# Routing search: counts by seventeen 32-column matmuls, one expansion from PSUM, the remaining capacity added by a matmul

## The chip, the cores and the metric

The kernel runs on one core of one Trainium2 chip. The metric is the device time of one execution in microseconds (us). Three runs of the kernel before took 782.95, 785.60 and 788.19 us, median 785.6 us. PE is TensorE (PEld its weight loads), DVE is VectorE, ACT is ScalarE, POOL is GpSimd, SP the engine that issues the plain loads.

## What is computed

Local and global attention over 8 batches gives 4608 tokens of 512 numbers. A gate gives each token 8 logits. A greedy routing by falling logit then gives each token one of 8 experts, each with room for 576 tokens, and each expert runs a two-layer net over its tokens.

```python
cap = N // E                                  # 4608 // 8 = 576
logits = x @ w_gate
order = np.argsort(-logits.flatten())
for idx in order:
    tok, e = (int(idx) // E, int(idx) % E)
    if assigned[tok] >= 0 or counts[e] >= cap:
        continue
    assigned[tok] = e
    counts[e] += 1
for e in range(E):
    mask = assigned == e
    h = np.maximum(x[mask] @ w1[e], 0.0)
    out[mask] = h @ w2[e]
```

## The kernel before, in words

Attention runs first. Then `experts` runs eight passes, one for each expert in the order in which the experts fill up. A pass is `ffn(ph)`: 16 groups of 12 matmuls (L853, moving 272 columns) into PSUM tile `H`, each evacuated by ACT (`hh`) and by DVE (`hl`), then 4 groups of 24 matmuls (L881, moving 512 columns) into `Y`.

Which expert fills next, and with which tokens, is found by `Routing.phase`. For seven of the eight phases it calls `search`, eight rounds of a 16-ary search for the logit at which some expert is full. A round is a chain between PE and DVE:

- A 0/1 table `G` (128 partitions x 34 token groups x 16 thresholds) is multiplied with the one-hot table `oh` (34 x 8 experts): five matmuls into PSUM tile `R` (variable `A`), four of them eight token groups wide (128 columns of `G`, 64 of `oh`) and the second one two groups wide (32 columns, 16). Only the diagonal blocks of the result are wanted.
- DVE masks out the diagonal blocks (`am`, from PSUM and the constant `dj`), reduces `am` to `C` (a ninth slice of `am` holds the remaining capacity of each expert), and spreads `C` over the 16 thresholds (`ce`, from `C` and `dk`).
- One matmul with the constant `big` sums `ce` over the partitions into PSUM tile `R2` (here called the sum matmul), DVE scans that for the threshold (`pm`), and `cand` builds the next `G`. A small `x` (the keys less the threshold found) is also made on DVE, ahead of `am` in its queue.

Phase 0 runs by itself after attention, since no expert can start without it. The routing of phase n+1 is woven into pass n. Every routing instruction on DVE goes through the helper `issue` (L405) and every routing matmul through `mm` (L468), so these two lines carry all of them in the profile; the tiles tell them apart.

The order is written out in advance: Tile follows the program order, and a small planner sets that order. `V.now` is its estimate of PE's time: each FFN matmul adds 117 ns (L853) or 216 ns (L881), each routing matmul 30 ns. `V.busy` is its estimate of when DVE is free: an instruction of n elements takes 130 ns plus 0.55 or 1.05 ns an element. `search` yields `ready()` = `V.busy` + 400 ns before its matmuls, so `step` places FFN matmuls on PE until the estimate has passed, and only then the routing matmul. What stands between a routing matmul and the next is so a fixed number of FFN matmuls, which cover the DVE chain as long as it is fast enough; PE takes its queue in order, so if DVE is late, PE stands still. The splits of the weights (`w1l`, `w2l`, L704) run on POOL all through the passes.

Of the kernel before, what the change touches and what calls it, by code (L numbers as in the profile page):

```python
# [21 lines left out]
E = 8  # L22
# [353 lines left out]
CU = 64  # L376
# [6 lines left out]
class Queue:  # L383
    """VectorE as the program order sees it: each instruction moves on an estimate of when the engine is free."""
# [24 lines left out]
class Routing:  # L409
# [10 lines left out]
    def prepare(s):  # L420
# [25 lines left out]
        s.dj = cf[:, CMISC:CMISC + 8]  # L446
        nc.vector.memset(s.am[:, 8], 0.0)
        nc.vector.memset(s.am[:16, 8], CU * (0.5 - CAP))
        nc.vector.memset(s.asgv, 0.0)
        nc.vector.tensor_copy(s.act, s.wt)  # L450
        s.dk = consts.tile([128, 16], F16, name="dk")
        nc.vector.tensor_copy(s.dk, cf[:, CMISC + 8:CMISC + 24])

    def begin(s, ctx):
# [4 lines left out]
        for n, w, dt in (("m", [34], F32), ("f", [34], I32), ("u", [34], I32), ("hi", [34], I32), ("mv", [34], F32),  # L459
                         ("v", [34, E], BF16), ("mo", [34], BF16), ("oh", [34, E], BF16), ("G", [34, 16], BF16),  # L460
                         ("asgv", [34], F32), ("act", [E], F32), ("am", [9, E], F16)):
# [5 lines left out]
    def mm(s, out, *args, **kw):  # L467
        s.nc.tensor.matmul(out, *args, **kw)  # L468
        s.V.now += 30
        s.V.busy = max(s.V.busy, s.V.now + 200)  # L470
# [36 lines left out]
    def search(s):  # L507
        nc = s.nc
        for it in range(NIT):
            yield -1  # L510
            yield s.V.ready()
            A = s.ps.tile([128, 8, E], F32, name="R")
            for i, j in enumerate((0, 4, 1, 2, 3)):
                n = 8 if j < 4 else 2
                s.mm(A[:16 * n, :n], s.G[:, 8 * j:8 * j + n].rearrange("p a b -> p (a b)"),
                                 s.oh[:, 8 * j:8 * j + n], start=(i == 0), stop=(i == 4))
# [6 lines left out]
            else:  # L523
# [15 lines left out]
            s.mm(p, s.big, ce, start=True, stop=True)  # L539
# [8 lines left out]
    def phase(s, ph):  # L548
# [40 lines left out]
        if more:  # L589
# [3 lines left out]
            s.V.tensor_tensor(ohg, s.oh, g[:, :, None].to_broadcast([128, 34, E]), op=ALU.mult)  # L593
        if not last:
# [63 lines left out]
        if more:  # L658
            s.V.tensor_tensor(rem, rem, cl[:16], op=ALU.min)
# [338 lines left out]
```

## Time and profile before

| what | us |
|---|---|
| median of three runs | 785.6 |
| lowest and highest | 782.95, 788.19 |
| span of the profiled execution | 797.1 |
| attention, up to the last gate reduction | 237.9 |
| first routing, up to the first FFN matmul | 282.8 |
| first L871 matmul of pass 0 and of pass 5 | 315.1, 658.0 |
| first L871 matmul of passes 6 and 7 | 709.1, 760.4 |

The profile gives the profiled execution's span and no other time of it; the span is 11.5 us above the median of the runs. A pass without routing takes 51.3 us (658.0 to 709.1 and 709.1 to 760.4). From pass 0 to pass 5 it is 68.6 us a pass (342.9 us for five), since routing stands in the same PE queue. In a timeline row stand start, duration, engine, line, operation, tiles, shape, count, and in brackets the engine's idle time before it with what ended it.

### The profile page before, as it was taken

What the parts mean: (1) busy time and instruction counts of PE and PEld (TensorE: products, weight loads), DVE (VectorE), ACT (ScalarE), POOL (GpSimd) and SP (SyncE); (2) the same over time, 40 slices, a digit from 0 to 9 for tenths busy, and PEclk for the clock granted to TensorE, in tenths of its full rate; (3) what the DMA queues carried; (4) which work ended last, traced back from release to release, by engine and by line L of the source; (5) the groups of instructions that cost most, each with busy time, mean ns of one, the idle gap of its engine ahead of it and who ended that gap; (6) DMA issues with size and microseconds to landing.
All of it is one profiled execution on the core that took longest, in us unless ns stands there. A gap on an engine that the chain in (4) does not pass through costs nothing.

```text
span 797.1 us, 19772 instructions
## 1 busy us (share of the span) xinstructions
PE 717.4 (90%) x7876; PEld 578.2 (73%) x7876; DVE 504.9 (63%) x1817; ACT 312.6 (39%) x849; POOL 319.3 (40%) x314
## 2 busy tenths in 40 slices
PE   7899999999982599989988988989899789999994
PEld 6677777777751488779668867858877787987973
DVE  6787887778776888579668667876875752121210
ACT  4656675756640143144223333332331323433410
POOL 5221111111000362566546655563653654574610
PEclk9999999999995579999999999999999999999998
DMA  9998889878310430601430440350341323332000
GB/s 354 406 342 295 327 296 318 314 261 313 142 69 1 145 123 1 264 35 34 143 135 28 150 157 18 120 178 28 120 162 44 119 57 123 132 119 87 28 20 36
DMA packets 32412, 120.42 MB, mean 151 GB/s; under 512 B 6720, under 2 KB 6976, under 8 KB 24128
## 3 DMA queue, kind: packets, MB, share of 16 engines
q1 hardware_dynamic: 22080, 67.78, 23.2%
q0 software_dynamic: 10240, 51.39, 18.6%
q8 instruction: 62, 1.02, 0.5%
q14 instruction: 30, 0.25, 0.1%
HBM read 101.32 MB, written 17.83 MB: 149 GB/s over the span
## 4 chain that ended last, share of the span: by engine, by line
PE 76%; DVE 14%; issue 3%; DMA 3%; POOL 1%; ACT 1%; another core or an unknown queue 0%; POOLq 0%; SPq 0%; ACTq 0%; DVEq 0%
PE Y L881 20%; PE H L853 19%; PE S L134 8%; PE R L468 6%; PE O L162 5%; PE T L150 4%; DVE r_G L405 3%; PE H L726 3%; PE S L195 2%; PE T L259 2%; DVE r_ce L405 2%; PE O L234 2%; PE T L224 2%; PE Y L871 2%; DMA w1r<-in_w_dram,widx 1%
## 5 line engine op out<-in xcount | busy, mean ns | idle before, releaser
L853 PE MATMUL H<-xh,w1h 128*128 128x272 f32 x512 | 153.4, 300 | 9.3 <-DVE hl L405 9.3
L853 PE MATMUL H<-xl,w1h 128*128 128x272 f32 x512 | 152.9, 299 | 0.0
L853 PE MATMUL H<-xh,w1l 128*128 128x272 f32 x512 | 152.5, 298 | 0.0
L405 DVE SCALAR_TENSOR_TENSOR hl<-H,hh 128x272 fp32r<-128x272 f32 x128 | 55.2, 435 | 90.4 <-ACT hh L855 59.7
L145 ACT ACTIVATE p<-p,nm 128x128 f32<-128x128 f32 x256 | 82.0, 394 | 67.5 <-DVE ls L165 34.7
L855 ACT ACTIVATE hh<-H 128x272 fp32r<-128x272 f32 x128 | 51.0, 398 | 145.7 <-PE H L853 138.8
L853 PEld LDWEIGHTS H<-xh,w1h 128*128 128x128 f32 x512 | 100.0, 195 | 10.6 <-DVE hl L405 10.2
L881 PE MATMUL Y<-w2h,hh 128*128 128x512 f32 x256 | 105.6, 412 | 0.0
L704 POOL TENSOR_TENSOR w2l<-w2r,w2h 128x512 fp32r<-128x512 f32 x64 | 82.0, 1304 | 58.8 <-ACT w2h L703 55.8
L704 POOL TENSOR_TENSOR w1l<-w1r,w1h 128x512 fp32r<-128x512 f32 x60 | 78.3, 1321 | 66.3 <-ACT w1h L703 66.1
L881 PE MATMUL Y<-w2h,hl 128*128 128x512 f32 x256 | 104.5, 408 | 0.0
L881 PE MATMUL Y<-w2l,hh 128*128 128x512 f32 x256 | 104.3, 407 | 0.0
L853 PEld LDWEIGHTS H<-xl,w1h 128*128 128x128 f32 x512 | 100.0, 195 | 0.3
L853 PEld LDWEIGHTS H<-xh,w1l 128*128 128x128 f32 x512 | 100.1, 195 | 0.0
L86 POOL COPY qz<-q 64x544 f32<-64x544 f32 x60 | 38.4, 639 | 151.6 <-DMA q<-in_qk_dram 118.5
L826 ACT ACTIVATE y<-Y 128x512 f32<-128x512 f32 (+1 forms) x40 | 23.1, 594 | 134.7 <-PE Y L881 83.1
L134 PE MATMUL S<-qk,qz 128*64 128x128 f32 x1024 | 70.5, 279 | 4.9 <-DVE qz L86 2.8
L134 PEld LDWEIGHTS S<-qk,qz 128*64 128x64 f32 x1024 | 54.9, 136 | 17.4 <-issue 11.3
L733 POOL DMA_INDIRECT out_dram<-y,idx x40 | 41.5, 1036 | 61.6 <-ACT y L826 29.7
L141 DVE CUSTOM_DVE_ANT_0 p<-S,mask 128x128 f32<-128x128 f32 x256 | 58.8, 286 | 6.4 <-PE S L134 4.5
L881 PEld LDWEIGHTS Y<-w2h,hh 128*128 128x128 f32 x256 | 49.2, 192 | 13.9 <-issue 4.2
L703 ACT ACTIVATE w1h<-w1r 128x512 fp32r<-128x512 f32 x64 | 38.3, 627 | 47.1 <-DMA w1r<-in_w_dram,widx 47.1
(165 smaller groups left out, 1273.1 us busy)
## 6 DMA issues: line engine op xcount, KB each, us to landing
vw<-in_vw_dram SPq DMA_DIRECT2D x32, 1040.0 KB, 8.3
qk<-in_qk_dram SPq DMA_DIRECT2D x32, 432.0 KB, 5.8
q<-in_qk_dram SPq DMA_DIRECT2D x32, 272.0 KB, 5.6
xd<-xs SPq DMA_DIRECT2D x8, 1024.0 KB, 7.1
xd<-xg SPq DMA_DIRECT2D x64, 8.0 KB, 5.9
xg<-xd,idx POOLq DMA_INDIRECT x40
out_dram<-y,idx POOLq DMA_INDIRECT x40
mask<-in_mask_dram SPq DMA_DIRECT2D x1, 512.0 KB, 5.7
```

Source lines behind the costliest of these rows:

```text
L86: eng.tensor_copy(z[r, :, h, :], q[r].rearrange("p (j i) -> p j i", i=32))
L134: nc.tensor.matmul(st[64 * r:64 * r + 64, c, :], z[:, j].rearrange("p h i -> p (h i)"), kw[:, k0:k0 + 128], start=True, stop=True)
L141: nc.vector.tensor_tensor_reduce(s.p[:, c, :], st[:, c, :], mask[:, 4 * s.u + c, :], 1.0, -BIG, ALU.add, ALU.max, nm[:, c:c + 1])
L145: nc.scalar.activation(s.p[:, c, :], s.p[:, c, :], AF.Exp, bias=nm[:, c:c + 1], scale=SCALE)
L162: nc.tensor.matmul(o[32 * r:32 * r + 32, k, h, :], s.pt[:, jj // 2, lo:lo + 32], vw[b, q][:, h, 8 * u + jj, :], start=True, stop=True)
L405: return op(*args, **kw)
L468: s.nc.tensor.matmul(out, *args, **kw)
L704: eng.tensor_tensor(lo, raw, hi, op=ALU.subtract)
L733: nc.gpsimd.indirect_dma_start(out=out, out_offset=bass.IndirectOffsetOnAxis(ap=rt.idx[ph][:n, t:t + 1], axis=0), in_=y[:n], in_offset=None)
L853: nc.tensor.matmul(p, w[d][:, fs], x[:, d, q], start=(d + k == 0), stop=(d + k == 5))
L855: nc.scalar.activation(hh[:, f, q], p, AF.Relu)
L881: nc.tensor.matmul(p, h[:, f, q], w[f], start=(f + k == 0), stop=(f + k == 9))
```

## The change

Three parts of `search` change, and what is tied to them.

- The counts: 17 matmuls of two token groups each (32 columns of `G`, 16 of `oh`), laid on four 32-partition strips of PSUM tile `R` by turns, in place of five. `R` is now 128 x 2 x 8.
- The expansion: one DVE `tensor_tensor` from PSUM (`ce`, 128 x 2 x 16 x 8, from `A` and the new constant `dk`) in place of `am`, `C` and `ce`. The sum matmul runs twice, once for each half of `ce`.
- The remaining capacity: kept in `rem` (128 x 16 x 8, partition 0 in use) and added by a third matmul with `big` that opens the sum in `R2`, right behind the 17.
- At the end of a phase `ohg` is first reduced on DVE (`cg`, 128 x 8), so one matmul with `ones` takes the place of five, and the reduction `c` behind them goes; `rem` is updated at 16 x 8 elements on one partition.
- The planner's price of a routing matmul goes from 30 to 60 ns, and is 20 ns for each of the 17.

```diff
-            A = s.ps.tile([128, 8, E], F32, name="R")
-            for i, j in enumerate((0, 4, 1, 2, 3)):
-                n = 8 if j < 4 else 2
-                s.mm(A[:16 * n, :n], s.G[:, 8 * j:8 * j + n].rearrange("p a b -> p (a b)"),
-                                 s.oh[:, 8 * j:8 * j + n], start=(i == 0), stop=(i == 4))
+            A = s.ps.tile([128, 2, E], F32, name="R")
+            for i in range(17):
+                j, r = slice(2 * i, 2 * i + 2), 32 * (i % 4)
+                s.mm(A[r:r + 32], s.G[:, j].rearrange("p a b -> p (a b)"), s.oh[:, j], ns=20, start=(i < 4),
+                     stop=(i >= 13))
+            p = s.ps.tile([128, 16, E], F32, name="R2")
+            s.mm(p, s.big, s.rem, start=True, stop=False)
...
-            C = s.t("C", [E], F16)
-            ce = s.t("ce", [16, E], F16)
-            s.V.tensor_tensor(s.am[:, :8], A, s.dj[:, :, None].to_broadcast([128, 8, E]), op=ALU.mult)
-            s.V.tensor_reduce(C, s.am.rearrange("p a b -> p b a"), axis=AX.X, op=ALU.add)
-            s.V.tensor_tensor(ce, C[:, None, :].to_broadcast([128, 16, E]),
-                                    s.dk[:, :, None].to_broadcast([128, 16, E]), op=ALU.mult)
+            ce = s.t("ce", [2, 16, E], F16)
+            s.V.tensor_tensor(ce, A[:, :, None, :].to_broadcast([128, 2, 16, E]),
+                              s.dk[:, :, :, None].to_broadcast([128, 2, 16, E]), op=ALU.mult)
             yield -1
             yield s.V.ready()
-            p = s.ps.tile([128, 16, E], F32, name="R2")
-            s.mm(p, s.big, ce, start=True, stop=True)
+            for k in range(2):
+                s.mm(p, s.big, ce[:, k], start=False, stop=(k == 1))
...
+            cg = s.t("cg", [E], BF16)
+            s.V.tensor_reduce(cg, ohg.rearrange("p a b -> p b a"), axis=AX.X, op=ALU.add)
...
-            pg = s.ps.tile([128, 8, E], F32, name="R")
-            for i, j in enumerate((0, 4, 1, 2, 3)):
-                n = 8 if j < 4 else 2
-                s.mm(pg[:, :n], s.ones, ohg[:, 8 * j:8 * j + n], start=(i == 0), stop=(i == 4))
+            pg = s.ps.tile([128, E], F32, name="R")
+            s.mm(pg, s.ones, cg, start=True, stop=True)
...
-            c = s.t("c", [E])
             cl = s.t("cl", [E])
-            s.V.tensor_reduce(c, pg.rearrange("p a b -> p b a"), axis=AX.X, op=ALU.add)
-            rem = s.am[:16, 8]
+            rem = s.rem[:1]
...
-    def mm(s, out, *args, **kw):
+    def mm(s, out, *args, ns=60, **kw):
         s.nc.tensor.matmul(out, *args, **kw)
-        s.V.now += 30
+        s.V.now += ns
```

What this does to the order is seen at three places. In the changed file the FFN lines stand two lower: L851 is the old L853, L879 the old L881. The first place is a round of the search on DVE, in the routing of phase 2 under pass 1. Before:

```order
L405 TENSOR_SCALAR r_x_5318<-r_x_5263,r_pm_5289 128x34
L405 TENSOR_TENSOR r_am<-R,cf 128x64
L405 TENSOR_REDUCE r_C<-r_am 128x8
L405 TENSOR_TENSOR r_ce<-r_C,dk 128x128
L405 SCALAR_TENSOR_TENSOR hl<-H,hh 128x272
L405 SCALAR_TENSOR_TENSOR r_pm_5346<-R_5344,fin 128x128
L405 SCALAR_TENSOR_TENSOR r_G<-r_x_5318,r_pm_5346,cf 128x544
```

The same round on DVE in the changed kernel:

```order
L405 TENSOR_SCALAR r_x_5437<-r_x_5371,r_pm_5392 128x34
L405 TENSOR_TENSOR r_ce<-R,dk 128x256
L405 SCALAR_TENSOR_TENSOR hl<-H,hh 128x272
L405 SCALAR_TENSOR_TENSOR r_pm_5458<-R_5435,fin 128x128
L405 SCALAR_TENSOR_TENSOR r_G<-r_x_5437,r_pm_5458,cf 128x544
```

Three instructions have become one, and an FFN evacuation (`hl`) still stands between it and the scan. The second place is PE under the `Y` matmuls of pass 4, in the routing of phase 5, from the last count matmul to the sum matmul. Before:

```order
L468 MATMUL R<-r_oh,r_G 128x64
L881 MATMUL Y<-w2h_4829,hh 128x512
L881 MATMUL Y<-w2l_4837,hh 128x512
L881 MATMUL Y<-w2h_4829,hl 128x512
L881 MATMUL Y<-w2h_4830,hh 128x512
L881 MATMUL Y<-w2l_4838,hh 128x512
L881 MATMUL Y<-w2h_4830,hl 128x512
L881 MATMUL Y<-w2h_4831,hh 128x512
L468 LDWEIGHTS big
L468 MATMUL R_8103<-r_ce,big 128x128
```

On PE in the changed kernel, from the matmul that adds `rem`:

```order
L468 MATMUL R_8530<-rem,big 128x128
L879 MATMUL Y<-w2l_4838,hh 128x512
L879 MATMUL Y<-w2h_4830,hl 128x512
L879 MATMUL Y<-w2h_4831,hh 128x512
L879 MATMUL Y<-w2l_4839,hh 128x512
L879 MATMUL Y<-w2h_4831,hl 128x512
L879 MATMUL Y<-w2h_4832,hh 128x512
L468 LDWEIGHTS big
L468 MATMUL R_8530<-r_ce,big 128x128
```

Seven `Y` matmuls as cover have become six (under the `H` matmuls twelve have become ten), and the last two rows stand there twice, once for each half of `ce`. From the sum matmul to the next counts it is 8 `Y` or 14 `H` matmuls in both kernels. The third place is PE under the `H` matmuls of pass 1, ahead of a sum matmul; a group of 12 begins with the row that has `xh` and `w1h_4818`. Before:

```order
L853 MATMUL H<-xh,w1h_4818 128x272
L853 MATMUL H<-xl,w1h_4818 128x272
L853 MATMUL H<-xh,w1l_4822 128x272
L853 MATMUL H<-xh,w1h_4819 128x272
L853 MATMUL H<-xl,w1h_4819 128x272
L853 MATMUL H<-xh,w1l_4823 128x272
L853 MATMUL H<-xh,w1h_4820 128x272
L468 LDWEIGHTS big
L468 MATMUL R_5513<-r_ce,big 128x128
```

In the changed kernel, on PE at the same place:

```order
L851 MATMUL H<-xh,w1h_4818 128x272
L851 MATMUL H<-xl,w1h_4818 128x272
L851 MATMUL H<-xh,w1l_4822 128x272
L851 MATMUL H<-xh,w1h_4819 128x272
L468 LDWEIGHTS big
L468 MATMUL R_5625<-r_ce,big 128x128
```

A round is now 10 + 14 = 24 `H` matmuls, exactly two groups, where it was 26. The sum matmul so falls behind the same place of a group in round after round (behind the fourth matmul in eight rounds, behind the third in seven), while before it moved on by two each round (behind the 5th, 7th, 9th, 11th).

More of the change, by code (lines that the diff above doesn't have):

```diff
@@ L445, in prepare @@
         s.fin = fin.rearrange("p i a b -> p i (a b)")
-        s.dj = cf[:, CMISC:CMISC + 8]
-        nc.vector.memset(s.am[:, 8], 0.0)
-        nc.vector.memset(s.am[:16, 8], CU * (0.5 - CAP))
+        s.rem = consts.tile([128, 16, E], F16, name="rem")
+        nc.vector.memset(s.rem, 0.0)
+        nc.vector.memset(s.rem[:1], CU * (0.5 - CAP))
         nc.vector.memset(s.asgv, 0.0)
         nc.vector.tensor_copy(s.act, s.wt)
-        s.dk = consts.tile([128, 16], F16, name="dk")
-        nc.vector.tensor_copy(s.dk, cf[:, CMISC + 8:CMISC + 24])
+        s.dk = consts.tile([128, 2, 16], F16, name="dk")
+        nc.vector.tensor_copy(s.dk, cf[:, CMISC:CMISC + 32].rearrange("p (a b) -> p a b", b=16))
     def begin(s, ctx):
@@ L647, in phase @@
         if more:
[L648 removed]
             cl = s.t("cl", [E])
[L650 to L651 removed]
+            rem = s.rem[:1]
             s.V.tensor_scalar(cl, s.wt, vs, -600.0 * CU, op0=ALU.is_equal, op1=ALU.mult)
[L653 removed]
+            s.V.scalar_tensor_tensor(rem, pg[:1, None, :].to_broadcast([1, 16, E]), float(CU), rem, op0=ALU.mult,
+                                     op1=ALU.add)
         idx = s.ix.tile([128, 5], I32, name="idx")
@@ L658, in phase @@
         if more:
-            s.V.tensor_tensor(rem, rem, cl[:16], op=ALU.min)
+            s.V.tensor_tensor(rem, rem, cl[:1, None, :].to_broadcast([1, 16, E]), op=ALU.min)
     def setup(s, j):
```

6 lines of the change are left out of this document (2 added, 4 removed).

## The prediction, made before the changed kernel was run

> **What bounds the kernel now.** I read the page first, then the windows by stage, then the timeline of one search round where the search runs alone and of one where it is woven into a pass.
>
> ```profile
> span 797.1 us, 19772 instructions
> ...
> PE 717.4 (90%) x7876; PEld 578.2 (73%) x7876; DVE 504.9 (63%) x1817; ACT 312.6 (39%) x849; POOL 319.3 (40%) x314
> ```
>
> PE is busy 90% of the span, but not alike everywhere. In the windows, the columns are length, busy time by engine, granted clock, DMA:
>
> ```profile
> 237.00:285.00 48.00, 21.79 (x142) 15.64 (x143) 34.82 (x115) 5.97 (x11) 10.28 (x10) 0.54 0.28 96
> ...
> 540.00:610.00 70.00, 66.78 (x447) 54.34 (x447) 48.76 (x127) 21.59 (x52) 35.77 (x31) 0.98 0.28 97
> ```
>
> In the first routing PE idles and the DVE/PE chain is the time: what a round loses there, the span loses. In the passes PE is full, so an added matmul costs its own time, and a shorter DVE chain gains only where PE had stood waiting for it. A round alone:
>
> ```profile
> 245.78 0.64 PE L468 MATMUL R<-r_oh,r_G 128*128 128x64 bf16 x5 [1.34 <-DVE r_G L405]
> 246.46 0.22 DVE L405 TENSOR_TENSOR r_am<-R,cf 128x64 f16<-128x64 f32 x1 [0.57 <-PE R L468]
> 246.72 0.28 DVE L405 TENSOR_REDUCE r_C<-r_am 128x8 f16<-128x72 f16 x1
> 247.03 0.29 DVE L405 TENSOR_TENSOR r_ce<-r_C,dk 128x128 f16<-128x128 f16 x1
> 247.38 0.29 PE L468 MATMUL R<-r_ce,big 128*128 128x128 f16 x1 [0.96 <-DVE r_ce L405]
> 247.71 0.42 DVE L405 TENSOR_TENSOR_SCAN r_pm<-R,fin 128x128 f32<-128x128 f32 x1 [0.38 <-PE R L468]
> 249.00 0.64 PE L468 MATMUL R<-r_oh,r_G 128*128 128x64 bf16 x5 [1.34 <-DVE r_G L405]
> ```
>
> It takes 3.22 us (245.78 to 249.00), of which 0.92 lies between `am` and the sum matmul. And a woven round, under the `Y` matmuls:
>
> ```profile
> 602.06 0.39 PE L881 MATMUL Y<-w2h,hl 128*128 128x512 f32 x1
> 602.29 0.51 PE L468 MATMUL R<-r_oh,r_G 128*128 128x64 bf16 x5
> 602.64 0.48 PE L881 MATMUL Y<-w2h,hh 128*128 128x512 f32 x1
> 602.95 0.39 PE L881 MATMUL Y<-w2l,hh 128*128 128x512 f32 x1
> 603.18 0.40 PE L881 MATMUL Y<-w2h,hl 128*128 128x512 f32 x1
> ...
> 603.41 0.29 DVE L405 TENSOR_TENSOR r_ce<-r_C,dk 128x128 f16<-128x128 f16 x1
> ...
> 604.35 0.23 PE L468 MATMUL R<-r_ce,big 128*128 128x128 f16 x1
> ```
>
> `ce` ends at 603.70 and its matmul starts at 604.35: 0.65 us to spare. The reader is to see that here the chain is hidden. It is not hidden where POOL is in the way:
>
> ```profile
> L405 DVE TENSOR_TENSOR r_ce<-r_C,dk x48: 291/293/3592, 285.6 to 619.6; 128x128 f16<-128x128 f16 x48
> ...
> L405 DVE TENSOR_TENSOR r_am<-R,cf x48: 210/225/226, 285.0 to 619.0; 128x64 f16<-128x64 f32 x48
> ...
> 424.15 3.39 DVE L405 TENSOR_TENSOR r_ce<-r_C,dk 128x128 f16<-128x128 f16 x1
> ...
> 423.66 3.73 POOL L704 TENSOR_TENSOR w2l<-w2r,w2h 128x512 fp32r<-128x512 f32 x3
> ...
> L468 PEld LDWEIGHTS <-big 128*128 128x128 f16 x48 | 4.7, 98 | 20.5 <-DVE r_ce L405 13.2 <-issue 5.6 <-DVE hl L405 0.8
> L468 PE MATMUL R<-r_oh,r_G 128*128 128x64 bf16 x188 | 22.0, 199 | 7.4 <-DVE r_G L405 7.4
> ```
>
> `ce` (minimum, median, maximum in ns) reads two SBUF operands and takes up to 3592 ns: the one at 424.15 ends at 427.54, as three splits on POOL end at 427.39. `am`, of the same operation but with an operand in PSUM, never passes 226 ns. PE waited 13.2 us for `ce` and 7.4 us for `G` in the passes.
>
> **The change, step by step.** The sum is made on the profiled span of 797.1 us; the runs' median, 785.6, is 11.5 lower, and I carry the difference over.
>
> *1. The first routing, 8 rounds.* `am`, `C`, `ce` and the way to PE take 0.92 (246.46 to 247.38). The new `ce` has 256 elements from PSUM. The nearest row:
>
> ```profile
> 225.30 0.42 DVE L170 TENSOR_TENSOR xs<-O,ls 128x256 f32<-128x256 f32 x1
> ...
> 219.28 0.66 PE L162 MATMUL O<-vw,pt 128*32 128x65 f32 x32
> ...
> L162 PE MATMUL O<-vw,pt x32: 220/220/244, 219.3 to 219.7; 128*32 128x65 f32 x32
> ...
> 511.80 0.98 PE L468 MATMUL R<-r_ohl,r_rhs 128*34 128x32 bf16 x13
> 512.72 0.32 PE L468 MATMUL R<-r_ohg,cb 128*128 128x64 bf16 x5
> ...
> 272.58 0.23 DVE L405 TENSOR_REDUCE r_c<-R 128x8 f32<-128x64 f32 x1
> 274.45 0.43 DVE L405 TENSOR_REDUCE r_mv<-r_v 128x34 f32<-128x272 bf16 x1
> ```
>
> So 0.42 + 0.06 to PE (247.32 to 247.38): 0.44 less. The 17 counts: `L162` has the same 32-column tiles, 32 in 0.66 us of which the last takes 0.22, so 0.014 each. At this stage's half clock that may be 0.028, 16 x 0.028 = 0.45, against 0.40 before (the five's 0.64 less some 0.24 for the last): 0.05 lost; but they move 16 columns, not 65, and at a quarter of that rate 0.29 is gained. I take 0.10 gained, nearer the row. The second sum matmul adds between nothing and the first one's 0.29; I take 0.10, since the five queued counts are at most 0.13 apiece. The one with `rem` runs while DVE makes `ce`, a cover of 0.48; without it, it would cost as much again. Per round -0.44 - 0.10 + 0.10 = -0.44, x 8 = -3.5. `cg` on DVE, a reduction of 272 elements like `r_mv`, adds 0.4 once, and `c` saves 0.2. Sum -3.3 (-5 to -2). Everything up to the first expert hangs on this, so it is gained in full.
>
> *2. More matmuls in the PE queue of the passes, 48 rounds.* Around the five counts two `Y` intervals of 0.23 become 0.89 (602.06 to 602.95): 0.43 for five, 0.35 of it up to the next `Y` (602.29 to 602.64) and 0.08 behind. Five full-width ones (`ohg`) take 0.32, the woven five 0.51: the difference, 0.19, belongs to the one 32-column matmul among them, two changes of tile shape at 0.1 each. The new order has two as well, in and out. Hence 0.19 + 17 x 0.014 + 0.08 = 0.51, 0.08 more; at a quarter of that rate 0.10 less. `rem` and the second sum matmul add 0.06 each (128 of the `Y` matmul's 512 columns at 0.23). So between 0.02 and 0.20; I take 0.17, nearer the row with the same tile: 48 x 0.17 = +8 (+1 to +13, the upper end with 0.13 for each `big` matmul). `pg` at each of five phase ends is one matmul instead of five: 4 x 0.03 (0.32 less 0.19 for the last, over four) x 5 = -0.6. `cg` there stands beside about 0.4 us more of FFN matmuls which the planner puts in for it: nothing.
>
> *3. PE's waits for `ce`.* They are 13.2 us. Short ones (`ce` at 0.9 to 1.1 us behind one split) go, since cover falls by 0.25 (12 `H` matmuls to 10) and the chain by 0.44 and POOL cannot hold it. Of long ones half comes back: `G` has two SBUF operands and follows some 1.5 us later, and three splits take 3.73. I take -8 (-13 to -4). The Trainium skill, page "SBUF — State Buffer", section "Who interferes with whom", says that a `tensor_tensor` contends with GpSimd's reads when both its inputs lie in SBUF, and that this port pair is the only place of contention among the engines. The rows of `ce` and `am` agree; by the rule alone the whole 13.2 would go and the sum below would be -6 instead of -1.4.
>
> *4. PE's waits for `G`.* Cover is the same 14 `H` or 8 `Y`, the chain longer by the second sum matmul. Late next is `hl`:
>
> ```profile
> 308.53 0.44 DVE L405 SCALAR_TENSOR_TENSOR hl<-H,hh 128x272 fp32r<-128x272 f32 x1 [0.36 <-ACT h L857]
> 308.96 0.42 DVE L405 TENSOR_TENSOR_SCAN r_pm<-R,fin 128x128 f32<-128x128 f32 x1
> 309.43 0.79 DVE L405 SCALAR_TENSOR_TENSOR r_G<-r_x,r_pm,cf 128x544 bf16<-128x544 f32 x1
> ...
> 308.70 0.23 PE L468 MATMUL R<-r_ce,big 128*128 128x128 f16 x1
> ...
> 310.58 0.51 PE L468 MATMUL R<-r_oh,r_G 128*128 128x64 bf16 x5
> ```
>
> Here the sum matmul stands behind the seventh of a group; `hl` of the group before waits for ACT until 308.53, holds the scan to 308.96, and `G` still ends 0.36 ahead of 310.58. Behind the fourth or third, the sum matmul comes three or four matmuls (0.38 to 0.50) sooner after that group, but `hl` does not, so the scan starts 0.3 to 0.5 later against PE's queue and the 0.36 is spent. Fifteen rounds stand so. Each then pays 0.1, and what POOL holds `G` for (994 ns on average below, against 783 at least) is no longer absorbed: 15 x 0.3 = +4.5 (0 to +9).
>
> ```profile
> L405 DVE SCALAR_TENSOR_TENSOR r_G<-r_x,r_pm,cf 128x544 bf16<-128x544 f32 x36 | 35.8, 994 | 1.3
> ...
> 428.30:431.70 3.40, 3.40 (x19) 3.19 (x18) 1.79 (x5) 0.92 (x2) 2.12 (x2) 0.50 0.00 0
> 431.70:435.00 3.30, 3.30 (x28) 3.12 (x26) 2.55 (x6) 1.45 (x5) 0.73 (x2) 0.99 0.22 82
> ```
>
> *5. The clock.* Behind the stall at 424.8 PE gets half the clock for 3.4 us and does 19 matmuls in place of 28: 1.5 us. One or two such stretches should go: -2 (-4 to +1).
>
> Sum: -3.3 + 8 - 0.6 - 8 + 4.5 - 2 = -1.4 us. 797.1 becomes 795.7, the median 784.
>
> **The rivals.**
>
> *The waits simply vanish.* `G` is not held longer and the stretches at half clock go: -3.3 + 5 - 0.6 - 13 + 1 - 4 = -15, 771 us. For it speaks that nothing in `ce` can be held; against it that `G`, `x` and `xl` still can.
>
> *The chain was hidden anyway.* Each wait for `ce` moves to the next `G`: -3.3 + 8 - 0.6 + 0 + 0 = +4, 790 us. The 0.65 us to spare at 604.35 speak for it; the 3.39 us `ce` against it.
>
> *The fixed alignment costs more (slower).* If `hl` holds the scan by 0.5 and every hold of `G` counts, 20 rounds x 0.45 = +9 instead of 4.5, with the matmuls at +13 and only -6 of waits gone: -3.3 + 13 - 0.6 - 6 + 9 - 1 = +11, 797 us. It decides once the scan starts over 0.36 later against its matmul than at 308.96.
>
> *The small matmuls do not overlap.* `r_rhs`, in 34-column loads, goes at 0.0625 each (0.98 less 0.23 over twelve). At that, 17 take 1.06 in place of 0.24: 48 x 0.82 + 8 x 0.6 = +44, 828 us. The `L162` row speaks against it. The Trainium skill, page "TensorEngine Tiling (Array Packing)", section "Restrictions" under the tile mapping, says column tiling disables the fast weight load, which would be this rival's cause; no row here tells a load's mode.
>
> **Chances.** The forecast 0.40, waits vanish 0.24, hidden anyway 0.15, alignment 0.14, no overlap 0.07. A change within 1% (7.9 us) is about what a measurement of this kernel cannot tell from none. Faster by more (under 777.7): most of the second case and a fifth of the first, 0.29. Slower by more (over 793.5): most of the alignment case, the last, a little of the third, 0.20. Within: 0.51. The range of 8 in 10 leaves out the last case and the outer ends: 771 to 797; the forecast's own is 777 to 791.
>
> **What would show it.** Right: a lone round near 2.8 us; `ce` never far over 0.42 us in the passes, and PE's wait for it near 3 to 5 us; about 0.6 from the first count to the next FFN matmul; the wait for `G` up from 7.4 towards 12. Wrong: 17 counts spread over 0.5 us or more, `ce` still stretched by POOL, or waits for `G` unchanged.

## The result, and the profile after

Over 20 runs each the changed kernel takes 790.66 us (788.45 to 795.05) and the kernel before 787.26 (781.01 to 794.86). The ratio is 1.0051, 95% interval 1.0028 to 1.0073: half a per cent slower, where 784 was forecast, a shade faster. The range of 771 to 797 holds the time; the sign is wrong.

The page of the changed kernel:

```profile
span 786.7 us, 21184 instructions
...
PE 715.7 (91%) x8636; PEld 579.5 (74%) x8636; DVE 487.2 (62%) x1705; ACT 312.9 (40%) x849; POOL 319.6 (41%) x314
```

This one profiled execution is shorter than that of before (797.1), though the runs say the opposite. A second profile of either kernel on another chip has spans of 793.6 (before) and 799.7 (changed). A sum over one pair of profiles can therefore not close to a few us; what follows uses what recurs in every profile of a kernel, and the timed ratios.

First the lone round, in the timeline of the changed kernel:

```profile
245.46 0.30 PE L468 MATMUL R<-r_oh,r_G 128*32 128x16 bf16 x17 [1.34 <-DVE r_G L405]
...
245.70 0.29 PE L468 MATMUL R<-rem,big 128*128 128x128 f16 x1
245.83 0.42 DVE L405 TENSOR_TENSOR r_ce<-R,dk 128x256 f16<-128x256 f32 x1 [0.26 <-PE R L468]
246.31 0.37 PE L468 MATMUL R<-r_ce,big 128*128 128x128 f16 x2 [0.32 <-DVE r_ce L405]
...
246.72 0.42 DVE L405 TENSOR_TENSOR_SCAN r_pm<-R,fin 128x128 f32<-128x128 f32 x1 [0.46 <-PE R L468]
...
248.02 0.30 PE L468 MATMUL R<-r_oh,r_G 128*32 128x16 bf16 x17 [1.34 <-DVE r_G L405]
```

A round is 2.56 us (245.46 to 248.02), where it was 3.22. The 17 counts take 0.30 us where five took 0.64, and `rem` runs while DVE makes `ce`. From the start of the last gate reduction (L275) to the first FFN matmul it is 40.7 us, where it was 45.2.

Then a woven round under the `Y` matmuls, PE alone:

```profile
595.62 0.39 PE L879 MATMUL Y<-w2h,hh 128*128 128x512 f32 x1
595.94 0.28 PE L468 MATMUL R<-r_oh,r_G 128*32 128x16 bf16 x17
596.16 0.23 PE L468 MATMUL R<-rem,big 128*128 128x128 f16 x1
596.20 0.48 PE L879 MATMUL Y<-w2l,hh 128*128 128x512 f32 x1
596.51 0.40 PE L879 MATMUL Y<-w2h,hl 128*128 128x512 f32 x1
...
597.44 0.40 PE L879 MATMUL Y<-w2h,hh 128*128 128x512 f32 x1
597.68 0.28 PE L468 MATMUL R<-r_ce,big 128*128 128x128 f16 x2
597.78 0.48 PE L879 MATMUL Y<-w2l,hh 128*128 128x512 f32 x1
598.09 0.39 PE L879 MATMUL Y<-w2h,hl 128*128 128x512 f32 x1
```

From the `Y` matmul ahead of the counts to the second one behind them it is 0.89 us (595.62 to 596.51), just what it was with five counts (602.06 to 602.95): 17 counts and `rem` cost PE no more than the five. Around the sum matmuls it is 0.65 (597.44 to 598.09), where one took 0.60 (604.11 to 604.71 in the kernel before).

Then the tiles `ce` and `G` (minimum, median, maximum in ns):

```profile
L405 DVE TENSOR_TENSOR r_ce<-R,dk x56: 408/424/427, 238.3 to 607.8; 128x256 f16<-128x256 f32 x56
...
L405 DVE SCALAR_TENSOR_TENSOR r_G<-r_x,r_pm,cf x42: 783/785/5451, 242.1 to 606.2; 128x544 bf16<-128x544 f32 x42
```

`ce`, which now reads PSUM and took up to 3592 ns before, stays at 0.42 us (427 ns at most) whatever POOL does. `G`, untouched by the change, went from at most 2162 ns to 5451. What PE waited for over the whole span (total, times, longest), kernel before:

```profile
PE R L468 <- DVE r_ce L405: 17.1, 17, 2.5
PE R L468 <- DVE r_G L405: 16.8, 14, 2.2
PE H L853 <- DVE hl L405: 9.3, 4, 4.3
```

and the changed kernel:

```profile
PE R L468 <- DVE r_G L405: 20.1, 14, 4.5
PE H L851 <- DVE hl L405: 12.7, 5, 4.3
...
PE R L468 <- DVE r_ce L405: 2.7, 8, 0.4
```

In this profile the waits for `ce` are gone but for the eight lone rounds; those for `G` and `hl` have grown, and the longest of them last 4.3 to 4.5 us. One of them, on three engines:

```profile
348.71 4.94 POOL L702 TENSOR_TENSOR w2l<-w2r,w2h 128x512 fp32r<-128x512 f32 x4
...
349.11 5.13 DVE L405 SCALAR_TENSOR_TENSOR r_G<-r_x,r_pm,cf 128x544 bf16<-128x544 f32 x1
...
349.86 0.29 PE L851 MATMUL H<-xl,w1h 128*128 128x272 f32 x1
...
354.16 0.43 DVE L405 SCALAR_TENSOR_TENSOR hl<-H,hh 128x272 fp32r<-128x272 f32 x1
...
354.30 0.30 PE L468 MATMUL R<-r_oh,r_G 128*32 128x16 bf16 x17 [4.15 <-DVE r_G L405]
```

Four splits run on POOL without a gap from 348.71 to 353.65. `G` starts under the first, and in place of 0.79 us takes 5.13: it ends only after the fourth. PE, with nothing left in front of the counts, stands for 4.15 us, and then has half its clock (the window behind it; the columns are length, busy time of PE, PEld, DVE, ACT and POOL, granted clock, DMA share and GB/s):

```profile
354.20:357.60 3.40, 3.31 (x32) 3.16 (x33) 1.53 (x6) 0.40 (x1) 0.89 (x1) 0.50 0.23 81
```

The same happens to a `G` at 415.92 (5.45 us), and to `pos`, 34 elements that take 0.195 us by the median:

```profile
484.67 5.41 DVE L405 SCALAR_TENSOR_TENSOR r_pos<-r_a,r_a 128x34 int32<-128x34 f32 x1
490.00 0.43 DVE L405 SCALAR_TENSOR_TENSOR hl<-H,hh 128x272 fp32r<-128x272 f32 x1
...
490.49 0.59 PE L851 MATMUL H<-xh,w1h 128*128 128x272 f32 x1 [4.31 <-DVE hl L405]
```

Here PE does not wait for the routing at all: `hl` queues behind `pos` on DVE, and the FFN matmul needs the PSUM tile that `hl` has not read yet. A second `pos`, at 548.85, takes 4.42 us. These four holds stand at the same places, with lengths within 0.02 us, in the second profile of the changed kernel; that of before repeats its own three likewise (`ce` 3.39 and 3.60, `rhs` 5.90). They come with the order, not by chance.

### The profile page after: what moved, and what is told of

It reads as the page before. It is cut to its first block, busy times and chain, and to the rows that moved or that the text cites. A ratio compares the mean times of both kernels' runs of the same rounds, so it can differ in the third digit from the quotient of the medians.

```text
span 786.7 us, 21184 instructions
## 1 busy us (share of the span) xinstructions
PE 715.7 (91%) x8636; PEld 579.5 (74%) x8636; DVE 487.2 (62%) x1705; ACT 312.9 (40%) x849; POOL 319.6 (41%) x314
## 4 chain that ended last, share of the span: by engine, by line
PE 79%; DVE 14%; issue 2%; DMA 2%; ACT 1%; POOL 0%; POOLq 0%; SPq 0%; ACTq 0%; DVEq 0%
PE Y L879 21%; PE H L851 21%; PE S L134 8%; PE R L468 6%; PE T L150 5%; PE O L162 4%; DVE r_G L405 3%; PE S L195 2%; PE T L259 2%; PE H L724 2%; PE Y L869 2%; PE O L234 2%; PE T L224 2%; DVE r_pos L405 1%; PE O L265 1%
## 5 line engine op out<-in xcount | busy, mean ns | idle before, releaser
L851 PE MATMUL H<-xh,w1h 128*128 128x272 f32 x512 | 156.3, 305 | 12.7 <-DVE hl L405 12.7
L851 PE MATMUL H<-xl,w1h 128*128 128x272 f32 x512 | 155.3, 303 | 0.0
L851 PE MATMUL H<-xh,w1l 128*128 128x272 f32 x512 | 154.5, 302 | 0.0
L851 PEld LDWEIGHTS H<-xh,w1h 128*128 128x128 f32 x512 | 102.9, 201 | 14.3 <-DVE hl L405 13.8
L853 ACT ACTIVATE hh<-H 128x272 fp32r<-128x272 f32 x128 | 50.8, 397 | 155.3 <-PE H L851 154.0
L879 PE MATMUL Y<-w2h,hh 128*128 128x512 f32 x256 | 103.6, 405 | 0.0
L879 PE MATMUL Y<-w2h,hl 128*128 128x512 f32 x256 | 103.4, 404 | 0.0
L879 PE MATMUL Y<-w2l,hh 128*128 128x512 f32 x256 | 103.2, 403 | 0.0
L851 PEld LDWEIGHTS H<-xl,w1h 128*128 128x128 f32 x512 | 102.6, 200 | 0.2
L851 PEld LDWEIGHTS H<-xh,w1l 128*128 128x128 f32 x512 | 102.7, 200 | 0.0
L879 PEld LDWEIGHTS Y<-w2h,hh 128*128 128x128 f32 x256 | 48.3, 189 | 14.0 <-issue 5.0
L879 PEld LDWEIGHTS Y<-w2l,hh 128*128 128x128 f32 x256 | 48.4, 189 | 9.1
```

The costliest lines, as they stand in the source:

```text
L851: nc.tensor.matmul(p, w[d][:, fs], x[:, d, q], start=(d + k == 0), stop=(d + k == 5))
L853: nc.scalar.activation(hh[:, f, q], p, AF.Relu)
L879: nc.tensor.matmul(p, h[:, f, q], w[f], start=(f + k == 0), stop=(f + k == 9))
```

## The experiments

All were timed in five rounds beside the kernel before on the same chip; the ratio is to that, with its 95% interval. "Holds" are DVE instructions over 2.5 us in the six passes with routing. A row of dots in a code cut marks lines that are left out.

**The two kernels once more.**

> The kernel before once more, for a second profile of it. Both theories: ratio 1.000 within 0.003. The first profile of before spans 797.1 us, above all its timed runs but one, while that of the changed kernel spans 786.7 us, below all of its own. If profiles scatter, this one should span some 785 to 790 us and show smaller sums of PE waits in the passes than the first; if profiling itself lengthens this kernel, it spans about 797 again.

> The changed kernel once more, for a second profile. Both theories: ratio to before 1.003 to 1.007. The first routing should again be 4 to 5 us shorter than before, and PE's waits in the passes should again be few and long: 4 to 5 us each, one per pass, under a run of four weight splits on POOL, and no longer at ce.

Measured: 0.9992 (0.9963 to 1.0021) and 1.0040 (1.0017 to 1.0063). The loss is real and of the same size on another chip.

**The planner's old prices, and the old order.** The first edit gives the changed kernel the prices of before (30 ns for each matmul; the 17 counts together 153, as five were 150; the three `big` matmuls together 30). The cover stays at 10 `H` or 6 `Y` ahead of the sum matmul, 14 or 8 behind it. The second edit also makes the planner believe that DVE is busy 204 ns longer behind `ce` (and not at all behind `cg`), which restores the cover of 12 or 7 and nearly the order of before.

```diff
-    def mm(s, out, *args, ns=60, **kw):
+    def mm(s, out, *args, ns=30, **kw):
...
-                s.mm(A[r:r + 32], ..., ns=20, ...)
+                s.mm(A[r:r + 32], ..., ns=9, ...)
-            s.mm(p, s.big, s.rem, start=True, stop=False)
+            s.mm(p, s.big, s.rem, ns=0, start=True, stop=False)
-                s.mm(p, s.big, ce[:, k], start=False, stop=(k == 1))
+                s.mm(p, s.big, ce[:, k], ns=15, start=False, stop=(k == 1))
...
-            s.mm(pg, s.ones, cg, start=True, stop=True)
+            s.mm(pg, s.ones, cg, ns=150, start=True, stop=True)
```

Of the second:

```diff
+            s.V.busy += 204
             yield -1
             yield s.V.ready()
...
```

What the next expectations call theory 'bursts' is called 'runs' in the later ones.

> The changed kernel with the planner's old prices for routing matmuls (150 ns for the counts with rem, 30 ns for the two sum matmuls, 30 ns for the rest); ten H matmuls still cover ce. Theory 'order' (the new order costs what the first routing gains): part of the loss goes if it came with the prices, ratio 0.995 to 1.000, and the two-group alignment that is left costs the rest. Theory 'bursts' (POOL's runs of splits catch the next DVE instruction with two SBUF operands whatever the order): no change, 1.003 to 1.007.

> As a_oldprice, and 204 ns added to the planner's estimate behind ce, none for cg, so that PE's queue has twelve H or seven Y matmuls between counts and sum matmul as before, nearly matmul for matmul: the new contents in the old order. Theory 'order': 4 to 8 us faster than before, ratio 0.990 to 0.995, with the alignment (5th, 7th, 9th, 11th matmul of a group) of before. Theory 'bursts': still no gain, ratio 1.000 to 1.006, with PE waits of 4 to 5 us under POOL's runs.

Measured: 0.9819 (0.9765 to 0.9874) and 0.9930 (0.9904 to 0.9955). The first gains more than either theory had allowed (its runs scatter, from 778.4 to 791.3 us); the second falls where theory 'order' had it. So the new contents gain 0.7% in the old order, and 1.8% at the old prices; the new prices turn this into a loss of 0.4%. The alignment does not carry the loss: the old-price kernel has the same 24 `H` matmuls a round, with the sum matmul behind the fourth of a group in ten rounds and behind the sixth in six, and PE's waits for `G` in it are 13.6 us, the longest 1.3. It has one hold, of 5.65 us; the changed kernel has four, 20.4 together. The old-order run fits less well: it has six holds, 22.0 us, and still gains. Holds cost only what their cover does not take up.

**Which of the prices.**

The two halves of the first edit above, each alone. The first takes only the default back, and keeps the search as the change has it:

```diff
-    def mm(s, out, *args, ns=60, **kw):
+    def mm(s, out, *args, ns=30, **kw):
...
-            s.mm(p, s.big, s.rem, start=True, stop=False)
+            s.mm(p, s.big, s.rem, ns=60, start=True, stop=False)
-                s.mm(p, s.big, ce[:, k], start=False, stop=(k == 1))
+                s.mm(p, s.big, ce[:, k], ns=60, start=False, stop=(k == 1))
...
```

The matmul of `pg` is kept at 60 in the same way.

The second has the search lines of the edit above (9, 0, 15 and 150 ns) and leaves the default at 60.

> The changed kernel with the old price of 30 ns for the matmuls outside the search alone (the 34 with rhs first of all); counts 20 ns each, rem, sum matmuls and pg 60 each as changed. Theory 'runs': the time goes with the DVE instructions over 2.5 us that the order brings about, about 1 us for each us of them: 0.982 with 6 us of them in all, 1.004 with 20. Theory 'order by the rest's price': this part of the price carries the loss, 0.980 to 0.988. Theory 'order by the search's price': 0.998 to 1.006.

> The converse: the search priced as before (17 counts 9 ns each, rem 0, the two sum matmuls 15 each, pg 150), the other matmuls at 60 ns. Theory 'runs': as above, 1 us for each us of DVE instructions over 2.5 us, from 0.982 at 6 us. Theory 'order by the search's price': 0.980 to 0.988. Theory 'order by the rest's price': 0.998 to 1.006.

Measured: 0.9988 (0.9958 to 1.0018), four holds, 16.8 us; and 0.9939 (0.9905 to 0.9973), two holds, 9.0 us. The second lies outside every range that was given for it, and neither part carries the loss by itself. The times of these four kernels stand in the order of the holds (20.4, 16.8, 9.0, 5.7 us to 1.004, 0.999, 0.994, 0.982), though not at 1 us for each.

**A gap between the splits (inconclusive).**

```diff
...
         nc.scalar.activation(hi, raw, AF.Copy)
+        if eng is nc.gpsimd:
+            nc.gpsimd.memset(gap, 0.0)
         eng.tensor_tensor(lo, raw, hi, op=ALU.subtract)
```

> The changed kernel with a memset of 128x32 on POOL ahead of each of its splits; the rows of PE, DVE and ACT stay the same, one for one. Theory 'runs' (a DVE instruction with two operands in SBUF waits until POOL's splits, run without a gap, are all done, and the changed order puts four such runs under G and pos): no DVE instruction of the passes over 2 us any more (four of 4.4 to 5.5 us before), the stalls of PE of about 4.5 us fall to 1 or less, ratio to the kernel before 0.980 to 0.990. Theory 'order' (the changed order costs by where matmuls stand, whatever POOL does): 1.000 to 1.007, as the changed kernel itself. If the long DVE instructions stay as long as they are, the memset does not part the splits, and the run tells nothing of the two.

> The changed kernel with the planner's old prices, and the same memset. Theory 'runs': the one DVE instruction of 5.65 us (hl of phase 4 under four splits) falls under 2 us, nothing else moves much: 0.975 to 0.981, where the old prices alone gave 0.982. Theory 'order': 0.980 to 0.985, as without the memset. The same caution on the memset holds.

Measured: 1.0093 (1.0058 to 1.0129) and 0.9872 (0.9837 to 0.9907). Each is some 0.5% above the same kernel without the memset. The memset does not part the splits; POOL and then DVE in the first of the two:

```profile
354.20 1.29 POOL L705 TENSOR_TENSOR w2l<-w2r,w2h 128x512 fp32r<-128x512 f32 x1
355.43 0.13 POOL L704 MEMSET gap<- 128x32 f32 x1
355.51 1.26 POOL L705 TENSOR_TENSOR w2l<-w2r,w2h 128x512 fp32r<-128x512 f32 x1
...
354.54 5.37 DVE L405 SCALAR_TENSOR_TENSOR r_G<-r_x,r_pm,cf 128x544 bf16<-128x544 f32 x1
```

By these rows the memset begins before the split ahead of it has ended, and `G` is held as long as before. As the expectation says, such a run tells nothing of the two theories.

**Splits cut short.** The order of PE, DVE and ACT is unchanged. From pass 1 on POOL's splits do 16 columns of 512, so these kernels leave out most of the low parts of the weights.

```diff
+        n = 16 if eng is nc.gpsimd and cur[0] > 0 else 512
-        eng.tensor_tensor(lo, raw, hi, op=ALU.subtract)
+        eng.tensor_tensor(lo[:, :n], raw[:, :n], hi[:, :n], op=ALU.subtract)
```

> The changed kernel, in which POOL's splits from pass 1 on do 16 columns in place of 512 (the low parts of the weights of later experts are so left at those of earlier ones; the splits of pass 0 are whole). The rows of PE, DVE and ACT stay the same, one for one. Theory 'runs' (POOL's unbroken runs of splits hold DVE, DVE holds PE, PE loses its clock): nothing on DVE lasts over 2 us from pass 1 on, the four stalls of PE of about 4.5 us go, and this kernel and op_thin lie within 0.7% of each other, both at 0.970 to 0.985 of the kernel before. Theory 'order' (where the matmuls stand costs it, whatever POOL does): this kernel stays 1.5% to 2.2% above op_thin.

> The changed kernel at the planner's old prices, with the same narrow splits. Theory 'runs': one hold of 5.6 us less than with the old prices alone, 0.970 to 0.980, and within 0.7% of a_thin. Theory 'order': 0.965 to 0.980, 1.5% to 2.2% under a_thin.

> The kernel before with the same narrow splits. Theory 'runs': its three holds of 3.4, 3.6 and 5.9 us go, 0.980 to 0.990; against it op_thin shows what the change's contents are worth where POOL holds nothing: 4.5 us less in the first routing, 2.9 more for the sum matmuls, little else, so op_thin 0 to 0.7% under it. If the contents gained by ce alone (theory 'ce': what counts is that POOL can no longer hold the expansion), op_thin would lie no more than 0.2% under b_thin.

Measured: 0.9566 (0.9518 to 0.9614), 0.9585 (0.9537 to 0.9634) and 0.9610 (0.9560 to 0.9661); medians 751.70, 753.76 and 754.64. All lie further down than either theory had it. Whole splits cost the kernel before 3.9%, the changed kernel nearly 5% (from 1.004) and the old-price kernel 2.4% (from 0.982). The point in dispute is plain: the 2.2% between new and old prices is gone (0.9566 against 0.9585, with intervals that overlap). The order that loses does so only where POOL's splits are long. The cut does not tell by which way: shorter splits also let POOL issue its transfers sooner. The passes with routing, from first `H` matmul to first `H` matmul (length, then busy time of PE, PEld, DVE, ACT and POOL, granted clock, DMA), in the kernel before, and then with its splits cut:

```profile
282.79:684.91 402.12, 372.95 (x2529) 310.25 (x2529) 272.52 (x691) 129.99 (x311) 213.13 (x182) 0.96 0.29 100
```

```profile
280.50:639.13 358.63, 357.51 (x2529) 300.64 (x2529) 227.02 (x691) 130.87 (x311) 124.37 (x182) 1.00 0.32 112
```

and in the changed kernel, whole and cut:

```profile
276.68:674.66 397.98, 372.53 (x3181) 311.87 (x3181) 256.54 (x595) 130.69 (x311) 213.78 (x182) 0.95 0.29 101
```

```profile
274.85:636.00 361.15, 358.23 (x3181) 299.54 (x3181) 214.24 (x595) 130.97 (x311) 126.07 (x182) 0.99 0.32 112
```

With the splits cut, PE idles 1 to 3 us in 360 and keeps its clock, in both. DVE's busy time falls by 42 to 46 us with the same instructions, so that much of it was waiting. PE's waits for `G` in the passes of the changed kernel are then 1.9 us, with its alignment as it was. And the changed kernel, where POOL holds little, loses 2.5 us in the passes against the kernel before (358.63 to 361.15) and gains 4.7 in the first routing (45.2 to 40.5).

**Splits set later.** The planner puts the next split once it reckons POOL free for 500 ns, not when POOL will be free within 200.

```diff
-AHEAD = 200
+AHEAD = -500
```

> The changed kernel with whole splits, the planner's prices as changed, but its rule for the next split set 700 ns later (it puts one where POOL has been free for 500 ns, not where it will be free in 200). Theory 'runs': if runs of three and four splits get rare, fewer holds over 2.5 us and 0.982 to 0.992; by the length of such holds, 1 us for each us from 0.982 at 6. Theory 'order': 0.998 to 1.006, since the prices stay.

> The changed kernel at the old prices with the later splits of the spaced run. Theory 'runs': by its holds over 2.5 us, 1 us for each us from 0.982 at 6, so 0.976 at none and 0.990 at 12. Theory 'order': the same gain as at the new prices (1.5%), 0.965 to 0.970.

Measured: 0.9892 (0.9842 to 0.9942) and 0.9876 (0.9828 to 0.9925). At the new prices it brings back 1.5%; unbroken runs of three or more splits from 285 us on fall from 18 to 2, the holds from 20.4 to 8.0 us. At the old prices it brings nothing (0.982 without), though such runs fall there too, from 13 to 3: the holds over 2.5 us are about as before, 6.4 us, but there are 30 instructions between 1.3 and 2.5 us in place of 21. Theory 'order' missed this run too. My price of 1 us for each us of long holds missed it, perhaps by leaving the shorter ones out.

**G out of POOL's reach.** The thresholds that `G` compares with are kept in PSUM, so that `G` has one large operand in SBUF and one in PSUM. The order stays.

```diff
+        s.rb = s.ps.tile([128, 4, 16 * E], F32, name="R2")
+        s.stp = s.rb[:, 1].rearrange("p (a b) -> p a b", b=16)
+        s.nc.vector.tensor_copy(s.stp, s.step)
...
-        t = s.step[:, it, None, :].to_broadcast([128, n, 16])
+        t = (s.step if sub is None else s.stp)[:, it, None, :].to_broadcast([128, n, 16])
...
-            p = s.ps.tile([128, 16, E], F32, name="R2")
+            p = s.rb[:, 0].rearrange("p (a b) -> p a b", b=E)
...
```

> The changed kernel, order and prices as they are, with the thresholds that G compares with kept in PSUM (a part of the bank of R2, written once), so that G reads one operand from SBUF and one from PSUM. Theory 'runs' (POOL's splits hold DVE instructions with two SBUF operands until a whole run is done): G never over 1 us in the passes, the two stalls of PE of 4.3 and 4.6 us at G go, those at pos (4.5 and 3.9) stay; 8 to 12 us less, ratio 0.988 to 0.996. Theory 'order' (POOL's load costs in some other way, the holds of G are not what counts): 1.000 to 1.008.

> The same at the planner's old prices, where no G lasted over 1.8 us, but many 1.4 to 1.8 in place of 0.79. Theory 'runs': small gain, 0.974 to 0.981 (0.982 without). Theory 'order': 0.980 to 0.986.

Measured: 0.9941 (0.9911 to 0.9970), against 1.004 to 1.005 without, and 0.9779 (0.9732 to 0.9826). Both fall where theory 'runs' had them; the second is not clear of the 0.982 without (0.9765 to 0.9874), so it does not part the theories. The tile `G` in the first of them, and what DVE does at the place of the stall shown above:

```profile
L405 DVE SCALAR_TENSOR_TENSOR r_G<-r_x,r_pm,R x42: 779/781/784, 241.7 to 596.6; 128x544 bf16<-128x544 f32 x42
```

```profile
348.22 0.78 DVE L405 SCALAR_TENSOR_TENSOR r_G<-r_x,r_pm,R 128x544 bf16<-128x544 f32 x1
349.19 0.44 DVE L405 SCALAR_TENSOR_TENSOR hl<-H,hh 128x272 fp32r<-128x272 f32 x1 [0.18 <-ACT h L858]
349.54 3.08 DVE L405 TENSOR_SCALAR r_x<-r_x,r_pm 128x34 f32<-128x34 f32 x1
352.54 0.41 DVE L405 TENSOR_TENSOR r_ce<-R,dk 128x256 f16<-128x256 f32 x1
```

`G` is through in 0.78 us under the same four splits. The next instruction that reads SBUF alone, the small `x`, is then held for the rest of them, and `ce` behind it is late: PE's wait is shortened from 4.15 to 2.08 us and handed on, not gone. Of the two holds of `pos` only one is left here (4.44 us), which was not foreseen, so not all of the gain need be that of `G`.

**The prices alone, on the old contents.** Five counts at 68 ns, the sum matmul at 180, the five of `pg` at 12, every other at 60.

```diff
-        s.V.now += 30
+        s.V.now += ns
...
-                                 s.oh[:, 8 * j:8 * j + n], start=(i == 0), stop=(i == 4))
+                                 s.oh[:, 8 * j:8 * j + n], ns=68, start=(i == 0), stop=(i == 4))
-            s.mm(p, s.big, ce, start=True, stop=True)
+            s.mm(p, s.big, ce, ns=180, start=True, stop=True)
...
```

> The kernel before with the changed prices: 340 ns for its five counts, 180 for its sum matmul, 60 for the five of pg together, 60 for every other routing matmul. Theory 'runs': the prices only shift where POOL's runs fall; the time goes with the holds over 2.5 us that the trace then shows (12.9 us of them in the kernel before), 1 us for each, and either sign can come out. Theory 'price': 1.015 to 1.022, as the prices cost the changed kernel.

Measured: 1.0169 (1.0121 to 1.0218). The prices lose 1.7% without any of the new contents. Both theories allowed this, so the run does not part them; it shows that the loss needs nothing else of the change. The holds are six, 24.4 us, against three, 12.9. The longest two fall on `x`, ahead of `am` in the queue; POOL and DVE:

```profile
419.27 4.98 POOL L704 TENSOR_TENSOR w2l<-w2r,w2h 128x512 fp32r<-128x512 f32 x4
...
419.29 5.01 DVE L405 TENSOR_SCALAR r_x<-r_x,r_pm 128x34 f32<-128x34 f32 x1
424.21 0.21 DVE L405 TENSOR_TENSOR r_am<-R,cf 128x64 f16<-128x64 f32 x1
```

**The contents alone, one order, G safe in both.** The edit of G in PSUM, on the kernel before and on the changed kernel in the old order.

> The kernel before, with G's thresholds in PSUM and nothing else. Its G is held for some 7 us in all above 0.79 each, much of it hidden; ce is still held twice, by 3.4 and 3.6 us, or by more if it now meets a run that G met first. Theory 'runs': 0.988 to 0.998. Theory 'order': 0.998 to 1.004.

> The changed kernel in the old order, with G's thresholds in PSUM. Without them it was at 0.993 with 13.1 us of G over 2.5 us each. Theory 'runs': those go, some come back at x or hl, 0.978 to 0.986, and 0.7% to 1.5% under b_psum, since ce can be held there and not here. If ce's protection is worth nothing once G is safe (theory 'hidden'), no more than 0.4% under b_psum.

Measured: 0.9901 (0.9867 to 0.9934) and 0.9755 (0.9723 to 0.9787), the second below its range. The contents are worth some 1.4% here (787.86 to 777.21 us). The first routing gives 4.4 of these 10.7 us (45.1 to 40.7). `ce` is held for 3.9 us in the one and never in the other (kernel before with G in PSUM, then the changed one):

```profile
L405 DVE TENSOR_TENSOR r_ce<-r_C,dk x56: 291/293/3933, 238.9 to 610.4; 128x128 f16<-128x128 f16 x56
```

```profile
L405 DVE TENSOR_TENSOR r_ce<-R,dk x56: 409/425/426, 239.2 to 603.3; 128x256 f16<-128x256 f32 x56
```

But PE's waits for `ce` in the passes are 6.9 and 6.7 us, so where the rest comes from is not shown: an instruction that is never held can still be late. This last version, at 0.9755, and the old-price kernel with G in PSUM, at 0.9779, beat both kernels of this study.

## Why the prediction was wrong

The sum had six terms, all for the new contents, and their net of -1.4 us had the sign that the contents have alone. In the old order they measure -0.7% (5.7 us), with `G` safe some -1.4%, and with the splits cut -0.1% to -0.4% (753.76 and 751.70 against 754.64). The step that failed is a term put at nothing without a reason: the planner's price of a routing matmul. I had it only as the length of cover. Taken back by itself, it moves the changed kernel from 1.004 to 0.982, some 17 us; put alone on the old contents, it costs 1.7%.

*1. The first routing, -3.3.* Measured -4.5, and 40.5 to 41.1 us in every kernel with the new contents against 45.0 to 45.3. `ce` at 0.42 was right. The term was too small because I let the 17 counts gain only 0.10; they gain 0.34 (0.64 to 0.30). A lone round is 2.56 where I had said near 2.8.

*2. More matmuls in the passes, +8.* Measured about +2.4: 48 x 0.05 for the second sum matmul, nothing for the 17 counts and `rem`. I had put each of the 17 at 0.014, as for the attention's matmuls of 65 columns; they take about 0.007 ((0.28 - 0.17) / 16, with 0.17 for the last). This is a size; whether the two changes of tile shape cost what I took for them is not separated. The upper bound of 13 was also too low by its own figures: 48 x (0.08 + 2 x 0.13) is 16. The -0.6 for `pg` was not measured by itself.

*3. PE's waits for `ce`, -8.* The 13.2 us that I started from are idle time of the weight loads (PEld); PE itself stood 9.4 us for `ce` in the passes. All of it went in the first profile; the second has 3.3 left (10.9 in the second of the kernel before). `ce` never passed 0.43 us, as the trace of `am` had promised. The rule that I had weighed there (the Trainium skill, "SBUF — State Buffer", section "Who interferes with whom") says that at most one SBUF input, outside the modes that use two ports, leaves a DVE instruction free of GpSimd. Every `ce` agrees, and so does every `G` of the runs in which it reads PSUM. The sum by that rule, with 13.2 in place of 8, would have been -6.6, not -6. That "half comes back" is not shown for `ce`; for a wait that leaves `G` the rows at 349.54 show it, handed to `x`.

*4. PE's waits for `G`, +4.5.* They rose by 3.3 us (16.8 to 20.1). That this is near the term is luck, since the reason is wrong. I had fifteen rounds pay 0.3 each because two groups of 12 make a round and `hl` holds the scan. What happened is two holds of 5.1 and 5.5 us. The kernel with old prices has the same rounds of 24 matmuls and waits 13.6 us for `G`, less than before.

*5. The clock, -2.* It went the other way: 0.96 before, 0.95 after, over the passes. Each of the changed kernel's four stalls of 3.8 to 4.5 us is followed by a stretch at a granted clock of 0.50, so a wait that moves brings its price with it. My 1.5 us for one such stretch was high by its own rows: 9 of 28 matmuls in 3.3 us are 1.1.

*What had no term.* `pos` and `hl`: the waits of the FFN itself for `hl` rose from 9.3 to 12.7 us. I had looked at what POOL does to the chain of a round, and not at the instructions at the end of a phase, which sit in the same DVE queue ahead of `hl`.

Of the rivals, "alignment costs more" ends slower, and "hidden anyway" stands at 790 us, near the 790.66 measured; neither is what happened. Against the alignment stand the old-price run and, with the order as it was, the changed kernel with its splits cut. And that the waits move on whole, as "hidden anyway" has it, fits the new order only: in the old order the same contents gain.

Why dearer matmuls bring longer holds is in part argued, not shown. A round under the `H` matmuls is 24 x 117 + 520 = 3328 ns for the planner at the new prices (17 x 20 + 60 + 120 for the search), and 24 x 117 + 183 = 2991 at the old. It puts a split for each 1225 ns, so 2.72 splits a round in place of 2.44, against the same FFN matmuls. On the chip 24 `H` matmuls, counts and sum matmuls take about 24 x 0.125 + 0.43 + 0.18 = 3.6 us, in which POOL does 2.9 splits of 1.25; once it is late, little slack is left for a gap. That setting the splits 700 ns later brought back 1.5% at the new prices fits this, but no run shows that it is the rate and not merely where the runs fall. Runs of three or more splits do not get more frequent with the prices on the old contents: 19 from 285 us on before, 18 with the new prices. What does rise is the number of runs of two or more splits that POOL begins late, over 0.1 us after ACT has made the first one's input: in the six passes from 4 to 7 on the old contents, and from 3 to 6 on the new. The old order has 7 of them and 22.0 us of holds and still gains, which stays open. Open too is whether the four holds cost the whole 2.2%: with two of them out of reach, 1.0% to 1.1% came back.

## What to carry to other kernels

A number that a scheduler uses is an edit like any other: ask which transfers and which other engine's work it moves, and give that a term, even where the instructions around the change keep their places. When one instruction is freed from another engine's port, list everything else in the same queue that still needs it, down to the 34-element ones, since the next of them inherits the wait. And before tuning a chain around such contention, cut the contender short once in an experiment: here it showed 3.9% to be had on the kernel before, where the change itself cost half a per cent.

## What the hardware showed that I had not expected

- A DVE instruction that meets POOL's splits can wait for a whole unbroken run of them: 5.13 us under four (4.94). The Trainium skill, page "SBUF — State Buffer", section "Who interferes with whom", speaks of a lock held for the whole instruction. Here it can last for the instructions that follow without a gap, and a memset of 0.12 us between them did not open it.
- Most instructions do not wait so long. In the same kernel a `G` that starts under the first of four splits is through when that one has ended:

```profile
290.08 5.51 POOL L702 TENSOR_TENSOR w2l<-w2r,w2h 128x512 fp32r<-128x512 f32 x4 [1.21 <-ACT w2h L701]
290.32 1.64 DVE L405 SCALAR_TENSOR_TENSOR r_G<-r_x,r_pm,cf 128x544 bf16<-128x544 f32 x1
```

- The two kinds can be told apart by whether POOL was late. In the fifteen traces with whole splits, a DVE instruction that reads SBUF alone met 260 unbroken runs of two or more splits. In the 199 whose first split began within 0.1 us of ACT ending its input (as at 290.08), none held it past the split that it met. In 54 of the other 61 one was held longer; the run at 348.71 began 2.02 us after its input was there. Why this is so, no run shows.
- Not only the splits hold. The `pos` at 484.67, whose median is 0.195 us, starts while POOL still issues a transfer (484.10 to 485.06), ahead of the first split at 485.08, and ends 5.41 us later.
- Not only instructions with two large operands are held. A `tensor_scalar` of 34 columns with one number per partition (`x`) took 5.01 us under a run of 4.98, and one with a single SBUF operand (`r_hl` from `r_pos`, median 0.18) is the 5.65 us hold of the old-price kernel. In which mode DVE ran it, no row tells.
- Seventeen matmuls of 32 x 16 columns on four strips took 0.30 us, also in the first routing, where the granted clock over 237 to 285 us was 0.61:

```profile
237.00:285.00 48.00, 25.14 (x298) 19.37 (x299) 36.21 (x101) 8.83 (x19) 14.53 (x14) 0.61 0.32 112
```
